# The attention's decay bias as a fourth product of the scores' matmul sum

## The chip, the cores and the metric

The kernel runs on one core of a Trainium2 chip. The metric is the device time of one execution in microseconds (us). Five engines run their own instruction streams in order and wait for each other on semaphores: PE (TensorE, matrix products), DVE (VectorE), ACT (ScalarE), POOL (GpSimd) and SP (SyncE, which here only issues DMAs).

## The reference, cut to what matters

Three layers follow each other: a causal attention with a decay bias, a mixture of eight experts whose gate is normalised eight times, and a two-matrix layer with softplus. The change lies in the attention alone:

```python
B, H, S, D = q.shape                     # 2, 8, 576, 64
scale = 1.0 / np.sqrt(D)                 # 1/8
scores = scale * np.matmul(q, k.transpose(0, 1, 3, 2))
causal = np.triu(np.ones((S, S), dtype=bool), k=1)
s_pos = np.maximum(s, 0.0)
cum = np.cumsum(s_pos, axis=-1)
bias = -(cum[:, :, :, None] - cum[:, :, None, :])
scores = np.where(causal, -1000000000.0, scores + np.minimum(bias, 0.0))
scores = scores - np.max(scores, axis=-1, keepdims=True)
attn = np.exp(scores)
attn = attn / (np.sum(attn, axis=-1, keepdims=True) + 1e-09)
return np.matmul(attn, v).astype(np.float32)
```

The bias of row r and column c is cum[c] - cum[r]. Where the mask lets a column through, it is never above zero, since cum only grows.

## The kernel before

Two heads form a pair (p = 0 to 7); head j of a pair stands on partitions 64j to 64j + 63 of q and k. The 576 rows of a head are cut into four blocks of 128 and a rest of 64. A unit (p, i) is row block i of both heads; i = 4 is the rest, both heads stacked on 128 partitions. So a pair has five units and the attention 40, numbered n = 0 to 39.

float32 operands are split into high bits and a rest (kh, kl, qh, ql), and the scores are the sum of three products, qh·kh + qh·kl + ql·kh, in PSUM (`scores`, L313 and L318; unit i = 0 takes one plain float32 product, L304). With c8 = 8·cum, DVE works out min(cum[c] - cum[r], 0) and the mask block by block into an SBUF tile `eb` (L366 and L367, for i = 4 L379 and L380). It needs c8 spread over all partitions (`cb`, a DMA from the DRAM scratch `c8d` that repeats each row 128 times, L223) and c8 as columns (`ccol`, made by TensorE transposes, L334 to L340). A custom DVE instruction (L371; L384 and L387 for i = 4) adds the scores to `eb` and takes the row's extreme; ACT takes the exponential (L399), DVE the sum's reciprocal (L408, L410), POOL scales the rows (L412), PE transposes them (L424, L430, L436), ACT takes them out of PSUM (L444), and PE multiplies by v (L456, L466).

The order is written by hand as a software pipeline. Step n issues, in this order: the last rest of a finished pair (Y), the scores of unit n + 1 (S), half a tile of the first expert's up-projection (U, L127, from step 28 on, four steps in five), the split of the next pair's k or q (K), v products of unit n - 5 (A), X, the evacuation of unit n - 4 (V), a piece of the first expert's weights (W), softmax of unit n with the reciprocals of unit n - 2 (B), the transposes of unit n - 3 (T), and the exponentials of unit n (E). The loads of the next pair follow at i = 1 (`load_rest`: cb, then v). After step 47 the experts' loop runs, in which PE has no pause.

PSUM has four score banks, so the scores of unit n + 1 wait for the row extremes of unit n - 1. The v tiles have two buffers, and SP issues in order: the v load of a pair stands in SP's queue until PE has done the last v product of the pair before the last one.

Of the kernel before, what the change touches and what calls it, by code (L numbers as in the profile page):

```python
# [10 lines left out]
F32 = mybir.dt.float32  # L11
# [9 lines left out]
def attention_moe_ffn(ctx, tc, q, k, v, s, w_gate, w1, w2, w_in, w_out, out):  # L21
# [41 lines left out]
    # The last layer's come as float64; as float32 they stand in DRAM scratch.  # L63
# [17 lines left out]
    def prep_steps(e, which, i, parts=1):  # L81
        """With more than one part, the rests are GpSimd's."""
        if e >= NE:
            return
        key = (e, which, i)
        t = raw_t.pop(key)
        hi = w_p.tile([P, WQ], F32R, tag=f"w{which}h", name=f"w{which}h")
        lo = w_p.tile([P, WQ], F32R, tag=f"w{which}l", name=f"w{which}l")
        c = KD if which == 1 else TQ
        wt[key] = (hi.rearrange("p (c n) -> p c n", c=c), lo.rearrange("p (c n) -> p c n", c=c))  # L90
        nc.scalar.activation(out=hi, in_=t, func=AF.Copy)  # L91
        for a in range(parts):
# [21 lines left out]
    def up_steps(e, g, ft, tag):  # L114
        """A generator: it stops halfway through the sum."""
# [28 lines left out]
        # a2: what 1 + a1 rounds away  # L144
# [17 lines left out]
    def down(e, g, t, tag):  # L162
        """A generator: it stops after each quarter of the sum."""
# [26 lines left out]
    with tc.manual_schedule():  # L190
        nc.scalar.preload_act_table_set("natural_log_exp_and_others")

# [1 line left out]
        with ExitStack() as att:  # L194
# [15 lines left out]
            def load(n):  # L210
                """Pair n // 2's k, then its q: both heads' rows."""
                p, r = divmod(n, 2)
                if p >= B * NP:
                    return
                b, hp = divmod(p, NP)
                x = ap2.tile([P, S], F32, tag="qk", name="qk", bufs=4)
                nc.sync.dma_start(out=x, in_=(q if r else k)[b, hp])
                qk_t.append(x)

            def load_rest(p):  # L220
                b, hp = divmod(p, NP)
                cb = ap2.tile([P, 2, S], F32, tag="cb", name="cb")
                nc.sync.dma_start(out=cb, in_=c8d[p:p + 1].to_broadcast([P, 2, S]))  # L223
                vv = ap2.tile([P, NB + 1, 2, D], F32, tag="vv", name="vv")
                hs = slice(2 * hp, 2 * hp + 2)
                nc.sync.dma_start(out=vv[:, :NB], in_=v[b, :NB * P, hs, :].rearrange("(c p) h d -> p c (h d)", p=P))
                nc.sync.dma_start(out=vv[:REM, NB], in_=v[b, NB * P:, hs, :])
                pair.setdefault(p, {}).update(vv=vv, cb=cb)
# [12 lines left out]
            c8d = dr.tile([B * NP, 2, S], F32, name="c8d")  # L241
            nc.sync.dma_start(out=c8d.rearrange("a j s -> (a j) s"), in_=c8)
# [8 lines left out]
            mask4 = ac.tile([P, REM], F32, name="mask4")  # L251
            nc.gpsimd.memset(mask4, 0.0)
            for j in range(2):
                r = slice(j * REM, (j + 1) * REM)
                nc.gpsimd.affine_select(out=mask4[r, :], in_=mask4[r, :], pattern=[[-1, REM]],
                                        compare_op=ALU.is_ge, fill=MASKED, base=0, channel_multiplier=1)

            ends = [[ac.tile([P, P], F32R, name=f"end{x}{y}") for y in "hl"] for x in range(2)]
            for x in ends:
                for y in x:  # L260
                    nc.gpsimd.memset(f(y), 0.0)

            def split(n, engine=nc.gpsimd):
                """Highest bits and the rest of load(n)."""
# [11 lines left out]
            def split_ends(p):  # L276
                """q's rows past the last whole block stand apart, head by head on the diagonal."""
# [16 lines left out]
            def scores(u):  # L294
# [3 lines left out]
                live[u] = dict(sc=sc)  # L298
                if i > 0:
                    kh, kl = t["kh"], t["kl"]  # L300
                else:
                    for j, x in enumerate(sc):
                        r = slice(j * D, (j + 1) * D)
                        nc.tensor.matmul(x[:, :P], qk_t[2 * p + 1][r, :P], qk_t[2 * p][r, :P], start=True, stop=True)  # L304
                    return
                if i < NB:
# [3 lines left out]
                    for n, (a, b) in enumerate(((qh, kh), (qh, kl), (ql, kh))):  # L310
                        for j, x in enumerate(sc):
                            r = slice(j * D, (j + 1) * D)
                            nc.tensor.matmul(x[:, :kp], a[r, qs], b[r, :kp], start=(n == 0), stop=(n == 2))  # L313
                else:
                    qh, ql = t["ends"]
                    for z, ks in ((sc[0][:, :S - 2 * P], slice(0, S - 2 * P)), (sc[1][:, :2 * P], slice(S - 2 * P, S))):
                        for n, (a, b) in enumerate(((qh, kh), (qh, kl), (ql, kh))):
                            nc.tensor.matmul(z, a, b[:, ks], start=(n == 0), stop=(n == 2))  # L318

            load_rest(0)  # L320
            ccol = ac.tile([P, NB, B * H], F32, name="ccol")
            ccol4 = ac.tile([P, B * H // 2], F32, name="ccol4")
            # the first row blocks' rows of c8, spread by TensorE
            cb0 = [ps.tile([P, 2, (i + 1) * P], F32, tag=f"y{i + 1}", name="cb0", bufs=1) for i in range(2)]

            def spread(i):
                for j in range(2):
                    nc.tensor.matmul(cb0[i][:, j, :], ident[:B * H, j:j + 1].to_broadcast([B * H, P]),
                                     c8[:, :(i + 1) * P], start=True, stop=True)

            spread(0)
            pc = ps.tile([P, NB + 1, B * H], F32, tag="tr", name="pc", bufs=2)
            for i in range(NB):
                nc.tensor.transpose(pc[:, i, :], c8[:, i * P:(i + 1) * P], ident[:B * H, :B * H])  # L334
            nc.tensor.transpose(pc[:REM, NB, :], c8[:, NB * P:], ident[:B * H, :B * H])
            spread(1)
            nc.vector.tensor_copy(ccol, pc[:, :NB, :])
            last = pc[:REM, NB, :].rearrange("p (a j) -> p j a", j=2)
            for j in range(2):
                nc.vector.tensor_copy(ccol4[j * REM:(j + 1) * REM, :], last[:, j, :])  # L340

# [9 lines left out]
            def softmax(u, before):  # L351
                """With `before`: the sums' reciprocals of the unit before, and what else waits."""
                p, i = u
                t, l = pair[p], live[u]
                cb, n = cb0[i] if p == 0 and i < 2 else t["cb"], 2 * p
                st = ap2.tile([P, 8], F32, tag="st", name="st", bufs=6)
                l["st"], l["eb"] = st, []
                if i < NB:
                    kk = (i + 1) * P
                    for j in range(2):  # L360
                        eb = eb_tile()
                        l["eb"].append(eb)
                        c, lo = ccol[:, i, n + j:n + j + 1], 0
                        if i > 1:
                            lo = i * P
                            nc.vector.tensor_scalar(eb[:, :lo], cb[:, j, :lo], c, 0.0, ALU.subtract, ALU.min)  # L366
                        nc.vector.scalar_tensor_tensor(out=eb[:, lo:kk], in0=cb[:, j, lo:kk], scalar=c,  # L367
                                                       in1=mask[:, W - kk + lo:], op0=ALU.subtract, op1=ALU.min)
                    for j, (eb, sc) in enumerate(zip(l["eb"], l["sc"])):
                        next(before, None)  # L370
                        nc.vector.tensor_tensor_reduce(eb[:, :kk], sc[:, :kk], eb[:, :kk], -0.125, BIG,  # L371
                                                       ALU.add, ALU.min, st[:, j:j + 1])
                else:
                    eb = eb_tile()
                    l["eb"].append(eb)
                    for j in range(2):
                        r = slice(j * REM, (j + 1) * REM)
                        c = ccol4[r, p:p + 1]
                        nc.vector.tensor_scalar(eb[r, :W], cb[r, j, :W], c, 0.0, ALU.subtract, ALU.min)  # L379
                        nc.vector.scalar_tensor_tensor(out=eb[r, W:], in0=cb[r, j, W:], scalar=c,  # L380
                                                       in1=mask4[r], op0=ALU.subtract, op1=ALU.min)
                    x, y = l["sc"]
                    next(before, None)
                    nc.vector.tensor_tensor_reduce(eb[:, S - 2 * P:], y[:, :2 * P], eb[:, S - 2 * P:], -0.125, BIG,  # L384
                                                   ALU.add, ALU.min, st[:, 4:5])
                    next(before, None)
                    nc.vector.tensor_tensor_reduce(eb[:, :S - 2 * P], x[:, :S - 2 * P], eb[:, :S - 2 * P], -0.125, BIG,  # L387
# [209 lines left out]
        # highest bits and rests side by side, their products are added up later  # L597
# [59 lines left out]
        # float64 words to float32; beyond float32's range they become 0 or its largest value.  # L657
        def convert(cv):
# [15 lines left out]
            for i, (_, dst) in enumerate(todo):  # L674
# [14 lines left out]
                # halves are rounded up: the highest bit that t has lost, times t's last place  # L689
# [8 lines left out]
        def turn(g):  # L698
            """The last layer's input: the experts' sum, transposed."""
# [73 lines left out]
def _parts(w, c):  # L773
    """[.., c * 128, n] in tiles with one run of memory for each partition: [.., 128, c, n]"""
# [5 lines left out]
def _columns(w, n):  # L780
    """[.., d, f] cut into blocks of n columns: [.., f / n, d, n]"""
# [4 lines left out]
def _pairs(a):  # L786
    """[B, H, S, D] as [B, H / 2, 2 * D, S]"""
# [33 lines left out]
```

## Time and profile before

| | |
|---|---|
| timed runs | 1143.37, 1143.65, 1145.00 us; median 1143.65 |
| span of the profiled execution, first to last instruction | 1142.8 us, 0.85 us below the median |
| busy in the span | PE 1120.3 us (98%), DVE 640.8 (56%), ACT 393.0 (34%), POOL 194.3 (17%) |
| attention, about 0 to 142 us | PE 123.7 us, DVE 123.0, ACT 94.7, POOL 84.7 |
| 8 loads of cb in it | 576 KB each, median 5.7 us from issue to landing |

The share of a whole span says little here: the attention is an eighth of it and has another limit than the experts. It is read by stretches of one pair.

### The profile page before, as it was taken

What the parts mean: (1) busy time and instruction counts of PE and PEld (TensorE: products, weight loads), DVE (VectorE), ACT (ScalarE), POOL (GpSimd) and SP (SyncE); (2) the same over time, 40 slices, a digit from 0 to 9 for tenths busy, and PEclk for the clock granted to TensorE, in tenths of its full rate; (3) what the DMA queues carried; (4) which work ended last, traced back from release to release, by engine and by line L of the source; (5) the groups of instructions that cost most, each with busy time, mean ns of one, the idle gap of its engine ahead of it and who ended that gap; (6) DMA issues with size and microseconds to landing.
All of it is one profiled execution on the core that took longest, in us unless ns stands there. A gap on an engine that the chain in (4) does not pass through costs nothing.

```text
span 1142.8 us, 15674 instructions
## 1 busy us (share of the span) xinstructions
PE 1120.3 (98%) x6037; PEld 993.1 (87%) x6037; DVE 640.8 (56%) x1316; ACT 393.0 (34%) x771; POOL 194.3 (17%) x234
## 2 busy tenths in 40 slices
PE   7789999999999999999999999999999999999998
PEld 5567788999999999999999999999999998999997
DVE  8998624644555465455546545554632357566653
ACT  5767622231223122122312212231221246565541
POOL 6675400000110111011011101101100012222220
PEclk9989999999999999999999999999999999999999
DMA  5432110220331223033122303312220112010001
GB/s 208 116 116 95 52 74 1 75 74 28 111 111 65 91 74 122 28 111 111 65 83 78 126 29 111 111 65 81 102 73 5 38 37 75 1 56 19 19 20 46
DMA packets 31210, 82.82 MB, mean 72 GB/s; under 512 B 5888, under 2 KB 10496, under 8 KB 31136
## 3 DMA queue, kind: packets, MB, share of 16 engines
q1 hardware_dynamic: 28576, 73.44, 19.7%
q0 software_dynamic: 2560, 8.39, 1.8%
q8 instruction: 47, 0.77, 0.3%
q14 instruction: 27, 0.22, 0.1%
HBM read 70.57 MB, written 10.78 MB: 71 GB/s over the span
## 4 chain that ended last, share of the span: by engine, by line
PE 92%; DVE 6%; issue 1%; DMA 1%; ACT 0%; ACTq 0%
PE ph L127 44%; PE py L174 44%; DVE eb L367 2%; DVE eb L371 1%; PE pv L456 1%; PE tr L430 1%; DVE eb L366 1%; PE sc L313 1%; DVE eb L379 1%; DVE st L408 0%; DVE eb L380 0%; PE pg L616 0%; PE px L703 0%; DMA cb<-c8d 0%; PE pv L466 0%
## 5 line engine op out<-in xcount | busy, mean ns | idle before, releaser
L127 PE MATMUL ph<-xh,w1h 128*128 128x384 f32 x960 | 325.2, 339 | 0.0
L127 PE MATMUL ph<-xl,w1h 128*128 128x384 f32 x960 | 322.4, 336 | 0.0
L127 PE MATMUL ph<-xh,w1l 128*128 128x384 f32 x960 | 322.4, 336 | 0.0
L133 DVE SCALAR_TENSOR_TENSOR hl<-ph,hh 128x384 fp32r<-128x384 f32 x192 | 106.6, 556 | 328.2 <-ACT hh L132 328.1
L174 PE MATMUL py<-w2h,hl 128*128 128x512 f32 x720 | 284.3, 395 | 0.0
L174 PE MATMUL py<-w2l,hh 128*128 128x512 f32 x720 | 283.6, 394 | 0.0
L174 PE MATMUL py<-w2h,hh 128*128 128x512 f32 x720 | 279.9, 389 | 0.0
L132 ACT ACTIVATE hh<-ph 128x384 fp32r<-128x384 f32 x192 | 94.5, 492 | 495.7 <-PE ph L127 495.5
L127 PEld LDWEIGHTS ph<-xh,w1h 128*128 128x128 f32 x960 | 180.3, 188 | 10.3 <-issue 0.7
L127 PEld LDWEIGHTS ph<-xl,w1h 128*128 128x128 f32 x960 | 180.3, 188 | 8.9
L127 PEld LDWEIGHTS ph<-xh,w1l 128*128 128x128 f32 x960 | 180.1, 188 | 0.0
L174 PEld LDWEIGHTS py<-w2h,hl 128*128 128x128 f32 x720 | 135.0, 187 | 28.6
L174 PEld LDWEIGHTS py<-w2l,hh 128*128 128x128 f32 x720 | 135.0, 187 | 22.5
L174 PEld LDWEIGHTS py<-w2h,hh 128*128 128x128 f32 x720 | 135.3, 188 | 22.0
L693 POOL TENSOR_TENSOR cm<-cm,ct 128x512 f32<-128x512 f32 x32 | 42.8, 1339 | 620.1 <-DVE ct L692 620.1
L147 POOL TENSOR_TENSOR a<-a,a 128x384 f32<-128x384 f32 x48 | 48.8, 1016 | 247.8 <-DVE a L145 247.8
L95 DVE TENSOR_TENSOR w2l<-raw,w2h 128x1024 fp32r<-128x1024 f32 x38 | 46.4, 1222 | 29.4 <-ACT w2h L91 29.4
L180 DVE SCALAR_TENSOR_TENSOR acc<-py,gate,acc 128x512 f32<-128x512 f32 x63 | 47.2, 749 | 19.5 <-PE py L174 19.4
L95 DVE TENSOR_TENSOR w1l<-raw,w1h 128x1024 fp32r<-128x1024 f32 x36 | 46.4, 1289 | 12.8 <-ACT w1h L91 11.8
L399 ACT ACTIVATE eb<-eb,st 128x128 f32<-128x128 f32 (+4 forms) x72 | 41.5, 579 | 31.9 <-DVE st L410 14.1
L412 POOL TENSOR_SCALAR eb<-eb,st 128x128 f32<-128x128 f32 (+4 forms) x72 | 43.2, 611 | 41.3 <-DVE st L410 27.5
L91 ACT ACTIVATE w2h<-raw 128x1024 fp32r<-128x1024 f32 x40 | 42.2, 1057 | 22.8 <-PE py L174 18.7
(146 smaller groups left out, 992.2 us busy)
## 6 DMA issues: line engine op xcount, KB each, us to landing
raw<-in_w SPq DMA_DIRECT2D x64, 512.0 KB, 5.5
f<-in_w_in SPq DMA_DIRECT2D x16, 512.0 KB, 4.4
f<-in_w_out SPq DMA_DIRECT2D x16, 512.0 KB, 3.5
wd<-cm POOLq DMA_DIRECT2D x32, 256.0 KB, 4.7
raw<-wd SPq DMA_DIRECT2D x16, 512.0 KB, 3.3
cb<-c8d SPq DMA_DIRECT2D x8, 576.0 KB, 5.7
qk<-in_k SPq DMA_DIRECT2D x8, 288.0 KB, 3.1
qk<-in_q SPq DMA_DIRECT2D x8, 288.0 KB, 3.2
```

Of the source, the lines that this page charges most:

```text
L91: nc.scalar.activation(out=hi, in_=t, func=AF.Copy)
L95: (nc.gpsimd if parts > 1 else nc.vector).tensor_tensor(out=lo[:, r], in0=t[:, r], in1=f(hi[:, r]), op=ALU.subtract)
L127: nc.tensor.matmul(ph, a, b, start=(n == 0), stop=(n == len(ops) - 1))
L132: nc.scalar.activation(out=hh, in_=ph, func=AF.Relu)
L133: nc.vector.scalar_tensor_tensor(out=hl, in0=ph, scalar=0.0, in1=f(hh), op0=ALU.max, op1=ALU.subtract)
L147: nc.gpsimd.tensor_tensor(out=a2, in0=a1, in1=a2, op=ALU.subtract)
L174: nc.tensor.matmul(py, x, y, start=(ft == 0 and n == 0), stop=(ft == NFT - 1 and n == 2))
L180: nc.vector.scalar_tensor_tensor(out=a, in0=py, scalar=gate_t[0][:, tt, e:e + 1], in1=a, op0=ALU.mult, op1=ALU.add)
L367: nc.vector.scalar_tensor_tensor(out=eb[:, lo:kk], in0=cb[:, j, lo:kk], scalar=c, in1=mask[:, W - kk + lo:], op0=ALU.subtract, op1=ALU.min)
L399: nc.scalar.activation(out=eb[:, :kk], in_=eb[:, :kk], func=AF.Exp, bias=st[:, j:j + 1], scale=-1.0, accum_out=st[:, 2 + j:3 + j])
L412: nc.gpsimd.tensor_scalar(eb[:, :kk], eb[:, :kk], st[:, 6 + j:7 + j], 1.0, ALU.mult, ALU.mult)
L693: nc.gpsimd.tensor_tensor(out=m, in0=m, in1=f(t), op=ALU.add)
```

## The change

The bias and the scores are both sums over products, so cum[c] - cum[r] is written as four more rows of a product. c8 is split into high bits and rest (`cs`, by ACT and DVE, once), and c8, its rest and both with the sign turned go to the DRAM scratch `c8d`. For each pair six small DMAs (`load_bias`) put two rows of 576 (or 64) values into the tiles bk, bq and be, whose other rows POOL has set to ones and zeros at the start (`init_bias`). `scores` then adds a fourth product, bq·bk (be·bk for i = 4), to each sum. DVE's bias blocks, the broadcast loads of cb and the columns `ccol` go; the custom instruction now adds the mask itself. The minimum with zero is no longer taken. The removed comments of the diff are left out here.

```diff
...
-                cb = ap2.tile([P, 2, S], F32, tag="cb", name="cb")
-                nc.sync.dma_start(out=cb, in_=c8d[p:p + 1].to_broadcast([P, 2, S]))
+                if p > 0:
+                    load_bias(p)
...
+            BB = 2
+            bq_t = [ac.tile([P, S], F32R, name=f"bq{x}") for x in range(BB)]
+            bk_t = [ac.tile([P, S], F32R, name=f"bk{x}") for x in range(BB)]
+            be_t = [ac.tile([P, P], F32R, name=f"be{x}") for x in range(BB)]
+
+            def init_bias(x):
+                for t in (bq_t[x], bk_t[x], be_t[x]):
+                    nc.gpsimd.memset(f(t), 0.0)
+                for j in range(2):
+                    for t, cols in ((bq_t[x], slice(0, S)), (bk_t[x], slice(0, S)),
+                                    (be_t[x], slice(j * REM, (j + 1) * REM))):
+                        nc.gpsimd.memset(f(t[j * D:j * D + 4, cols]), 1.0)
+
+            def load_bias(p):
+                for j in range(2):
+                    h = 2 * p + j
+                    nc.sync.dma_start(out=f(bk_t[p % BB][j * D + 2:j * D + 4, :]), in_=c8d[h, 0:2, :])
+                    nc.sync.dma_start(out=f(bq_t[p % BB][j * D:j * D + 2, :]), in_=c8d[h, 2:4, :])
+                    nc.sync.dma_start(out=f(be_t[p % BB][j * D:j * D + 2, j * REM:(j + 1) * REM]),
+                                      in_=c8d[h, 2:4, NB * P:])
...
-            c8d = dr.tile([B * NP, 2, S], F32, name="c8d")
-            nc.sync.dma_start(out=c8d.rearrange("a j s -> (a j) s"), in_=c8)
+            init_bias(0)
+            cs = [eb_tile(B * H, f"cs{x}").bitcast(F32R) for x in range(4)]
+            c8d = dr.tile([B * H, 4, S], F32, name="c8d")
+            for a, b in ((0, 2 * P), (2 * P, S)):
+                x = c8[:, a:b]
+                nc.scalar.activation(out=cs[0][:, a:b], in_=x, func=AF.Copy)
+                nc.scalar.activation(out=cs[2][:, a:b], in_=x, func=AF.Copy, scale=-1.0)
+                nc.vector.tensor_tensor(out=cs[1][:, a:b], in0=x, in1=f(cs[0][:, a:b]), op=ALU.subtract)
+                nc.vector.tensor_tensor(out=cs[3][:, a:b], in0=f(cs[0][:, a:b]), in1=x, op=ALU.subtract)
+            for x in range(4):
+                nc.sync.dma_start(out=c8d[:, x, :], in_=f(cs[x]))
+            load_bias(0)
...
-                        nc.tensor.matmul(x[:, :P], qk_t[2 * p + 1][r, :P], qk_t[2 * p][r, :P], start=True, stop=True)
+                        nc.tensor.matmul(x[:, :P], qk_t[2 * p + 1][r, :P], qk_t[2 * p][r, :P], start=True, stop=False)
+                    for j, x in enumerate(sc):
+                        r = slice(j * D, (j + 1) * D)
+                        nc.tensor.matmul(x[:, :P], bq[r, :P], bk[r, :P], start=False, stop=True)
...
-                    for n, (a, b) in enumerate(((qh, kh), (qh, kl), (ql, kh))):
+                    for n, (a, b) in enumerate(((qh, kh), (qh, kl), (ql, kh), (bq, bk))):
...
-                        for n, (a, b) in enumerate(((qh, kh), (qh, kl), (ql, kh))):
-                            nc.tensor.matmul(z, a, b[:, ks], start=(n == 0), stop=(n == 2))
+                        for n, (a, b) in enumerate(((qh, kh), (qh, kl), (ql, kh), (be, bk))):
+                            nc.tensor.matmul(z, a, b[:, ks], start=(n == 0), stop=(n == 3))
...
-            spread(0)
...
-                        if i > 1:
-                            lo = i * P
-                            nc.vector.tensor_scalar(eb[:, :lo], cb[:, j, :lo], c, 0.0, ALU.subtract, ALU.min)
-                        nc.vector.scalar_tensor_tensor(out=eb[:, lo:kk], in0=cb[:, j, lo:kk], scalar=c,
-                                                       in1=mask[:, W - kk + lo:], op0=ALU.subtract, op1=ALU.min)
...
-                        nc.vector.tensor_tensor_reduce(eb[:, :kk], sc[:, :kk], eb[:, :kk], -0.125, BIG,
+                        nc.vector.tensor_tensor_reduce(eb[:, :kk], sc[:, :kk], mask[:, W - kk:], -0.125, BIG,
...
```

Two places show how the instructions stand. The first is DVE, softmax of unit i = 3 (the v and norm work of other units stands between; st holds a row's extreme, sum and reciprocal). Before:

```order
L366 TENSOR_SCALAR eb<-cb,ccol 128x384
L367 SCALAR_TENSOR_TENSOR eb<-cb,ccol,mask 128x128
L366 TENSOR_SCALAR eb<-cb,ccol 128x384
L367 SCALAR_TENSOR_TENSOR eb<-cb,ccol,mask 128x128
L408 TENSOR_SCALAR st<-st 128x2
L371 ISA eb,st<-sc,eb 128x512
L371 ISA st 128x1
L410 RECIPROCAL st<-st 128x2
L371 ISA eb,st<-sc,eb 128x512
```

And in the changed kernel, where the line numbers are those of its own file:

```order
L412 TENSOR_SCALAR st<-st 128x2
L381 ISA eb,st<-sc,mask 128x512
L381 ISA st 128x1
L414 RECIPROCAL st<-st 128x2
L381 ISA eb,st<-sc,mask 128x512
```

The four bias instructions in front of the unit are gone; the custom instruction reads the mask where it read eb. The second place is SP's queue from one pair's v load to the bias of the next pair. Before:

```order
L226 DMA vv<-in_v 128x4x128
L227 DMA vv<-in_v 64x128
L78 DMA raw<-in_w 128x1024
L287 DMA end0h<-qh 64x64 x2
L287 DMA end0l<-ql 64x64 x2
L217 DMA qk<-in_k 128x576
L217 DMA qk<-in_q 128x576
L223 DMA cb<-c8d 128x1152
```

In the changed kernel:

```order
L226 DMA vv<-in_v 128x4x128
L227 DMA vv<-in_v 64x128
L78 DMA raw<-in_w 128x1024
L322 DMA end0h<-qh 64x64 x2
L322 DMA end0l<-ql 64x64 x2
L217 DMA qk<-in_k 128x576
L217 DMA qk<-in_q 128x576
L248 DMA bk_95<-c8d 2x576
L249 DMA bq_93<-c8d 2x576
L250 DMA be_97<-c8d 2x64
L248 DMA bk_95<-c8d 2x576
L249 DMA bq_93<-c8d 2x576
```

One DMA has become six (the sixth, be of the second head, follows). Before, it was DVE's softmax that waited for this load; now it is PE, whose scores stand first in a step.

## Rows read from the trace of the kernel before

**Rows 1.** The chain that ended last, in order of time: start, us, what.

```profile
142.17 4.36 PE ph L127 x24
```

**Rows 2.** Stretches: length, busy PE PEld DVE ACT POOL, PEclk, DMA share, GB/s.

```profile
32.36:48.36 16.00, 11.81 (x114) 8.46 (x113) 15.92 (x51) 11.46 (x31) 11.29 (x15) 1.00 0.47 131
48.36:64.46 16.10, 13.34 (x113) 9.51 (x114) 16.02 (x51) 11.28 (x31) 10.49 (x14) 0.89 0.40 130
64.46:79.65 15.19, 14.14 (x113) 10.26 (x113) 15.11 (x51) 11.87 (x32) 10.93 (x15) 0.78 0.43 138
...
96.54:111.86 15.32, 15.32 (x139) 11.92 (x138) 13.00 (x52) 11.19 (x33) 8.13 (x11) 1.00 0.20 63
```

**Rows 3.** Timeline of PE, 93 to 110 us: start, duration, instruction.

```profile
93.13 0.39 PE L318 MATMUL sc<-kh,end1h 128*128 128x320 f32 x1
...
96.96 0.44 PE L127 MATMUL ph<-xh,w1h 128*128 128x384 f32 x1
...
98.21 0.95 PE L466 MATMUL pv<-pt,vv 128*64 128x64 f32 x20
...
99.89 0.28 PE L313 MATMUL sc<-kl,qh 64*128 64x256 f32 x2
100.01 0.29 PE L313 MATMUL sc<-kh,ql 64*128 64x256 f32 x2
...
106.57 0.40 PE L313 MATMUL sc<-kl,qh 64*128 64x512 f32 x2
106.80 0.39 PE L313 MATMUL sc<-kh,ql 64*128 64x512 f32 x2
```

**Rows 4.** Groups of DVE, 32.36 to 79.65 us: busy, mean ns, idle before.

```profile
L367 DVE SCALAR_TENSOR_TENSOR eb<-cb,ccol,mask 128x128 f32<-128x128 f32 (+1 forms) x24 | 16.1, 691 | 0.0
...
L366 DVE TENSOR_SCALAR eb<-cb,ccol 128x256 f32<-128x256 f32 (+1 forms) x12 | 8.6, 717 | 0.0
...
L379 DVE TENSOR_SCALAR eb<-cb,ccol 64x512 f32<-64x512 f32 x6 | 3.3, 548 | 0.0
...
L380 DVE SCALAR_TENSOR_TENSOR eb<-cb,ccol,mask 64x64 f32<-64x64 f32 x6 | 2.3, 386 | 0.0
```

**Rows 5.** Timeline of PE, 20 to 147 us; in brackets the idle time before.

```profile
48.36 0.48 PE L304 MATMUL sc<-qk 64*128 64x128 f32 x2 [0.45 <-DVE st L371]
...
50.82 0.63 PE L424 MATMUL tr<-ident,eb 128*128 128x128 f32 x4 [0.42 <-ACT pt L444]
...
52.59 0.44 PE L456 MATMUL pv<-pt,vv 128*64 128x128 f32 x4 [0.37 <-DVE xl L530]
...
132.10 0.44 PE L456 MATMUL pv<-pt,vv 128*64 128x128 f32 x4 [1.29 <-DVE xl L530]
```

**Rows 6.** Timeline of SP's queue, 0 to 150 us: start, time to issue, DMA.

```profile
0.74 0.40 SPq L231 DMA_DIRECT2D s_sb<-in_s  x1
1.20 0.41 SPq L217 DMA_DIRECT2D qk<-in_k  x1
...
50.44 0.38 SPq L226 DMA_DIRECT2D vv<-in_v  x1
...
55.69 0.38 SPq L223 DMA_DIRECT2D cb<-c8d  x1
```

**Rows 7.** Timeline of all engines, 0 to 17 us.

```profile
1.26 0.52 POOL L248 MEMSET mask<- 128x512 f32 x1
...
4.78 0.33 SPq L242 DMA_DIRECT2D c8d<-c  x1
4.95 1.40 POOL L274 TENSOR_TENSOR kl<-qk,kh 128x576 fp32r<-128x576 f32 x1 [1.24 <-ACT kh L273]
...
7.21 0.34 SPq L223 DMA_DIRECT2D cb<-c8d  x1
...
14.31 0.89 POOL L412 TENSOR_SCALAR eb<-eb,st 128x128 f32<-128x128 f32 x2 [1.14 <-DVE st L410]
...
16.67 0.58 PE L304 MATMUL sc<-qk 64*128 64x128 f32 x1 [0.25 <-DVE st L371]
```

More of the change, by code (lines that the diff above doesn't have):

```diff
@@ L227, in load_rest @@
                 nc.sync.dma_start(out=vv[:REM, NB], in_=v[b, NB * P:, hs, :])
-                pair.setdefault(p, {}).update(vv=vv, cb=cb)
+                pair.setdefault(p, {}).update(vv=vv)
+            BB = 2
[16 more added lines that the diff above has]
+                                      in_=c8d[h, 2:4, NB * P:])
             s_sb = eb_tile(B * H, "s_sb")
@@ L250, in attention_moe_ffn @@
                                     compare_op=ALU.is_ge, fill=MASKED, base=0, channel_multiplier=1)
-            mask4 = ac.tile([P, REM], F32, name="mask4")
+            mask4 = ac.tile([P, S], F32, name="mask4")
             nc.gpsimd.memset(mask4, 0.0)
@@ L254, in attention_moe_ffn @@
                 r = slice(j * REM, (j + 1) * REM)
-                nc.gpsimd.affine_select(out=mask4[r, :], in_=mask4[r, :], pattern=[[-1, REM]],
+                nc.gpsimd.affine_select(out=mask4[r, W:], in_=mask4[r, W:], pattern=[[-1, REM]],
                                         compare_op=ALU.is_ge, fill=MASKED, base=0, channel_multiplier=1)
@@ L261, in attention_moe_ffn @@
                     nc.gpsimd.memset(f(y), 0.0)
+            for x in range(1, BB):
+                init_bias(x)
             def split(n, engine=nc.gpsimd):
@@ L298, in scores @@
                 live[u] = dict(sc=sc)
+                bq, bk, be = bq_t[p % BB], bk_t[p % BB], be_t[p % BB]
                 if i > 0:
@@ L309, in scores @@
                     qh, ql = t["qh"], t["ql"]
-                    for n, (a, b) in enumerate(((qh, kh), (qh, kl), (ql, kh))):
+                    for n, (a, b) in enumerate(((qh, kh), (qh, kl), (ql, kh), (bq, bk))):
                         for j, x in enumerate(sc):
                             r = slice(j * D, (j + 1) * D)
-                            nc.tensor.matmul(x[:, :kp], a[r, qs], b[r, :kp], start=(n == 0), stop=(n == 2))
+                            nc.tensor.matmul(x[:, :kp], a[r, qs], b[r, :kp], start=(n == 0), stop=(n == 3))
                 else:
@@ L316, in scores @@
                     for z, ks in ((sc[0][:, :S - 2 * P], slice(0, S - 2 * P)), (sc[1][:, :2 * P], slice(S - 2 * P, S))):
-                        for n, (a, b) in enumerate(((qh, kh), (qh, kl), (ql, kh))):
-                            nc.tensor.matmul(z, a, b[:, ks], start=(n == 0), stop=(n == 2))
+                        for n, (a, b) in enumerate(((qh, kh), (qh, kl), (ql, kh), (be, bk))):
+                            nc.tensor.matmul(z, a, b[:, ks], start=(n == 0), stop=(n == 3))
             load_rest(0)
[L321 to L329, printed above, removed]
-            spread(0)
[L332 to L340, printed above, removed]
             scores(units[0])
@@ L353, in softmax @@
                 p, i = u
-                t, l = pair[p], live[u]
-                cb, n = cb0[i] if p == 0 and i < 2 else t["cb"], 2 * p
+                l = live[u]
                 st = ap2.tile([P, 8], F32, tag="st", name="st", bufs=6)
@@ L359, in softmax @@
                     kk = (i + 1) * P
-                    for j in range(2):
+                    for j, sc in enumerate(l["sc"]):
                         eb = eb_tile()
                         l["eb"].append(eb)
-                        c, lo = ccol[:, i, n + j:n + j + 1], 0
-                        if i > 1:
-                            lo = i * P
-                            nc.vector.tensor_scalar(eb[:, :lo], cb[:, j, :lo], c, 0.0, ALU.subtract, ALU.min)
-                        nc.vector.scalar_tensor_tensor(out=eb[:, lo:kk], in0=cb[:, j, lo:kk], scalar=c,
-                                                       in1=mask[:, W - kk + lo:], op0=ALU.subtract, op1=ALU.min)
-                    for j, (eb, sc) in enumerate(zip(l["eb"], l["sc"])):
                         next(before, None)
-                        nc.vector.tensor_tensor_reduce(eb[:, :kk], sc[:, :kk], eb[:, :kk], -0.125, BIG,
+                        nc.vector.tensor_tensor_reduce(eb[:, :kk], sc[:, :kk], mask[:, W - kk:], -0.125, BIG,
                                                        ALU.add, ALU.min, st[:, j:j + 1])
@@ L375, in softmax @@
                     l["eb"].append(eb)
[L376 to L381, printed above, removed]
                     x, y = l["sc"]
                     next(before, None)
-                    nc.vector.tensor_tensor_reduce(eb[:, S - 2 * P:], y[:, :2 * P], eb[:, S - 2 * P:], -0.125, BIG,
+                    nc.vector.tensor_tensor_reduce(eb[:, S - 2 * P:], y[:, :2 * P], mask4[:, S - 2 * P:], -0.125, BIG,
                                                    ALU.add, ALU.min, st[:, 4:5])
                     next(before, None)
-                    nc.vector.tensor_tensor_reduce(eb[:, :S - 2 * P], x[:, :S - 2 * P], eb[:, :S - 2 * P], -0.125, BIG,
+                    nc.vector.tensor_tensor_reduce(eb[:, :S - 2 * P], x[:, :S - 2 * P], mask4[:, :S - 2 * P], -0.125, BIG,
                                                    ALU.add, ALU.min, st[:, 5:6])
```

## The prediction

> **What bounds the kernel now.** The chain that ended last is PE's from 142.17 us on [rows 1]; only the attention, before that, can move the end. I read it first by stretches of one pair. From 32 to 80 us DVE is busy for 15.92 of 16.00, 16.02 of 16.10 and 15.11 of 15.19 us, while ACT has 11.3 to 11.9, POOL 10.5 to 11.3 and PE 11.8 to 14.1 us [rows 2]: DVE paces the first half. From 96.54 on PE is busy for all of 15.32 us and DVE for 13.00: with the expert's up-projection between the units, PE paces the second half. PE's timeline dates the turn: the first-half pace holds until the scores of unit 29 (p = 5, i = 4) at 93.13, behind which the first up-projection follows [rows 3].
>
> **Part 1: DVE's bias blocks go.** Over three pairs they take 16.1 + 8.6 + 3.3 + 2.3 = 30.3 us [rows 4], 10.1 a pair. DVE's 15.9 a pair becomes about 5.8. Nothing is added on DVE in the loop: the custom instruction reads the mask in place of eb, in the same shape, and I cost that at nothing. DVE falls far below the others, so the question is what is late next.
>
> **Part 2: the pace of the first half without DVE.** Four candidates, a pair each:
> - ACT keeps all its work: (11.46 + 11.28 + 11.87)/3 = 11.5 us [rows 2].
> - POOL: (11.29 + 10.49 + 10.93)/3 = 10.9 us [rows 2].
> - PE at full clock: 15.32 us hold four pieces of up-projection; one takes 98.21 - 96.96 = 1.25 us [rows 3], so 15.32 - 5.0 = 10.3 us are attention. The fourth product costs, by start-to-start distances, 0.12 us for the two heads at 256 columns and 0.23 at 512 [rows 3]. Between these I take 0.12 for 128 columns, 0.17 for 384, and 0.15 and 0.12 for the stacked unit's 320 and 256. Sum 0.12 + 0.12 + 0.17 + 0.23 + 0.27 = 0.91 us: 11.2 a pair.
> - SP's ring: the scores of a pair now wait for the pair's bias rows, whose DMAs stand behind the v load in SP's queue, and that load waits for PE in the step of the scores of the pair before. From scores at 48.36 [rows 5] to the v load at 50.44 are 2.1 us, from there to the load of cb at 55.69 are 5.25 [rows 6]. PE needs the first five of six DMAs for the unit i = 0; at 0.46 us from issue to issue (0.74 to 1.20 [rows 6]) the fifth starts 1.8 us later, and a small transfer through DRAM took 7.21 - 4.78 = 2.4 us until its reader could go [rows 7]. Ring: 2.1 + 5.25 + 1.8 + 2.4 = 11.6 us.
>
> The four lie between 10.9 and 11.6. Where one engine paces, the others' waits hide; with four so near, each in order, part of their waits adds up. PE's waits that DVE's blocks don't cause, on ACT's evacuation and on xl, are 0.42 + 0.37 us in one pair [rows 5]. I take 11.5 + 0.8 = 12.3 us a pair; the floor is 11.5, the upper bound today's pace.
>
> Between the scores of unit 5 at 16.67 [rows 7] and those of unit 29 at 93.13 [rows 3] lie 24 steps, 4.8 pairs, 15.9 us each. At 12.3 they take 59.0 in place of 76.5 us: 17.5 us less.
>
> **Part 3: the start.** Two costs lie on the path to unit 5.
> - c8 must be split and go through DRAM. Before, its DMA starts at 4.78 [rows 7]; now four subtractions by DVE on 16 rows come first, 1.5 us at the 386 ns of the smallest group and 2.8 at the 691 of the largest [rows 4]. I take 1.5, since nothing else runs on DVE. The last of the four DMAs goes at 6.3, has landed at 8.7, the fifth bias DMA starts 1.8 later and takes 2.4: 12.9 us for the scores of unit 0, or up to 0.7 less where the issues overlap; I take 12.2.
> - POOL sets the bias tiles before its first kl. One set is six memsets of 576 columns, by the 0.52 us of the mask's 512 [rows 7], and three small ones: 3.6 us; two sets and the wider mask are about 7.5. POOL's first kl moves from 4.95 to about 11.5, and since the next kl and ql (1.4 us each [rows 7]) and the split by ACT stand before POOL's first scaling of rows, that goes from 14.31 to about 17.5, the first transposes to about 18.5, and the scores of unit 5, behind them on PE, to about 19.2 in place of 16.67. Lag 2.5 us, between 0 and 5.
>
> The spread by TensorE and the columns ccol go too; they lie before unit 0, which now waits for the DMAs anyway, so I count no gain.
>
> **Part 4: the second half.** PE paces it and gets the fourth product of units 29 to 39: two pairs at 0.91 and one stacked unit at 0.27, 2.1 us more. PE's one large pause, 1.29 us before 132.10, ends on xl by DVE, which stood behind the last bias blocks [rows 5]; it goes. Net 0.8 us more. From there on the same instructions run, only earlier.
>
> **Parts off the path.** The eight broadcasts of cb (576 KB each) go and 48 small DMAs come. Their price is in SP's ring; the bytes saved help raw and qk land, which nothing waits for long now, so zero, with 1 us either way.
>
> **Sum.** -17.5 + 2.5 + 0.8 = -14.2 us on the profiled span of 1142.8, which lies 0.85 below the median run: 1143.65 - 14.2 = 1129.5 us.
>
> **TensorE's clock** is the unknown. The granted clock was 1.00 in one pair of the first half, 0.89 and 0.78 in the next two, with PE pausing on DVE, and 1.00 where PE was never idle [rows 2]. [...]
>
> **Rivals.**
> 1. PE stays at a mixed clock. At the 0.78 of the third pair, 11.2 us of PE work become 14.4 a pair and PE paces. 4.8 × (15.9 - 14.4) = 7.2 less 3.3 gives 1139.8 us. For it: the two dips, and that the first half still has no up-projection to fill PE. Against it: where PE had 100% the clock stayed at 1.00, and PE now has 91% to do at that level.
> 2. ACT alone paces, without added waits, at 11.5, and the lag at the start hides behind it: 4.8 × 4.4 = 21 - 1.5 - 0.8 gives 1125 us. For it: the steps have one unit of slack everywhere. Against it: in-order waits of four engines.
> 3. Slower: the bias rows land late. PE stands in front of the scores of unit i = 0 until the fifth small DMA has landed, and everything behind it on PE (v products, transposes) stands too. The ring is 11.6 us at 2.4 us to land. It reaches today's pace at 6.7 us, and since 3.3 us are lost anyway, the change is slower once a transfer takes over 6.0: the ring is then above 15.2. At 7.4, as behind the raw weights and two loads of qk that stand in front in the queue, it would be 16.6, so 4.8 × 0.7 + 3.3 = 6.7 us slower, 1150 us. For it: cb took 5.7 us in the median. Against it: cb moved 576 KB, these some 5 KB.
> 4. It doesn't remove the limit: the row extremes still run on DVE behind the reciprocals of unit n - 2, which wait for ACT, and the pace stays near 15.5: 4.8 × 0.4 - 3.3 is about 1 us slower, 1145 us. Against it: ACT has 11.5 us to do in 16 and so keeps two units ahead once DVE lets it.
>
> **How the numbers follow.** Chances: the forecast (pace 12 to 13, 1126 to 1134 us) 0.55; rival 1 and everything between 13 and 15 (1134 to 1142) 0.25; rival 2 and better (1120 to 1126) 0.12; rival 3 0.05; rival 4 0.03. The time is the forecast's, 1129.5 us. The range for 8 in 10 runs from 1121, below rival 2, to 1139, which takes in most of rival 1. A difference counts from 0.2% on, 2.3 us, about what a measurement of this kernel can tell from no change: faster 0.91 (the forecast, rival 2, nearly all of rival 1), the same 0.04, slower 0.05.
>
> **What would show it.** Right: DVE about 6 us busy per pair until the first up-projection and ACT over 90%; scores of unit 29 near 78 us (19.2 + 59.0); granted clock 0.95 or more; bias products 0.23 us for two heads at 512 columns; unit 5's scores near 19 us; the second half within 1 us of the 49 us between 93.13 and 142.17 [rows 1, 3]. Rival 1 shows as L127-free pairs of 14 us and more with PE without pauses at a low clock; rival 3 as PE waiting on the bias DMAs before each unit i = 0; rival 4 as ACT idle on DVE. The prediction is wrong if the pace lies outside 11.3 to 13.8 us a pair, or if something after the attention starts to wait on loads that no longer have their lead.

## The result, and the profile after

The changed kernel takes 1125.82 us (median of four runs: 1125.42, 1125.47, 1126.17, 1128.16) beside 1144.13 for the kernel before on the same chip: ratio 0.9844, 95% interval 0.9830 to 0.9858. The forecast was 1129.5, range 1121 to 1139. The gain is 18.3 us by the medians; the profiled spans (1142.8 and 1123.6 us) differ by 19.2.

The page of the changed kernel has PE on 98% of the chain, and DVE at 585.9 us, 54.9 less than before.

```profile
## 1 busy us (share of the span) xinstructions
PE 1107.6 (99%) x6104; PEld 987.7 (88%) x6104; DVE 585.9 (52%) x1189; ACT 393.1 (35%) x775; POOL 197.1 (18%) x252
...
PE 98%; POOL 1%; ACT 0%; issue 0%; DVE 0%; POOLq 0%; ACTq 0%
```

These stretches of the changed kernel, from one pair's first scores to the next's, answer to [rows 2] (length, then busy time of PE, PEld, DVE, ACT, POOL with counts, PEclk, DMA share, GB/s). The fifth holds one piece of up-projection, the sixth several.

```profile
19.49:30.49 11.00, 11.00 (x105) 8.38 (x104) 8.46 (x40) 10.96 (x33) 11.00 (x17) 1.00 0.26 82
30.49:41.87 11.38, 11.38 (x125) 8.85 (x124) 7.06 (x34) 11.13 (x32) 10.32 (x16) 1.00 0.45 133
41.87:53.45 11.58, 11.41 (x124) 8.85 (x123) 7.42 (x34) 11.07 (x32) 9.19 (x14) 1.00 0.44 131
53.45:64.83 11.38, 11.38 (x124) 8.85 (x123) 5.63 (x27) 10.94 (x31) 10.07 (x16) 1.00 0.42 133
64.83:77.53 12.70, 12.70 (x130) 9.96 (x129) 7.85 (x33) 10.68 (x33) 9.53 (x14) 1.00 0.40 120
77.53:93.73 16.20, 16.20 (x148) 12.79 (x147) 7.35 (x35) 11.40 (x33) 7.67 (x11) 1.00 0.09 25
```

PE's column equals the length in all but one stretch, where 0.17 us are missing: from unit 5 on PE paces the attention, the first half too. DVE has fallen from 15.9 us a pair to between 5.6 and 8.5. ACT and POOL are close behind PE. The granted clock is 1.00 in all six, where [rows 2] had 0.89 and 0.78.

PE's timeline dates the same points as [rows 3, 5, 7]: the scores of unit 5, of unit 29, and the first piece of the expert loop that PE runs to the end.

```profile
19.49 0.71 PE L340 MATMUL sc<-qk 64*128 64x128 f32 x3
...
73.85 0.39 PE L357 MATMUL sc<-kh,end1h 128*128 128x320 f32 x1
...
122.17 0.95 PE L470 MATMUL pv<-pt,vv 128*64 128x64 f32 x20
123.05 0.44 PE L127 MATMUL ph<-xh,w1h 128*128 128x384 f32 x1
```

| stretch | before | after | difference | forecast |
|---|---|---|---|---|
| start to the scores of unit 5 | 16.67 | 19.49 | +2.8 | +2.5 |
| unit 5 to unit 29, 4.8 pairs | 76.46 (15.9 a pair) | 54.36 (11.33 a pair) | -22.1 | -17.5 |
| unit 29 to the end of the attention | 49.0 | 49.2 | +0.2 | +0.8 |
| sum | | | -19.1 | -14.2 |

So the direction and the order of the terms held, and the large term was too small by 4.6 us.

### The profile page after: what moved, and what is told of

The parts are those of the page before. It is cut to its first block, busy times and chain, and to the rows that moved or that the text cites. A ratio compares the mean times of both kernels' runs of the same rounds, so it can differ in the third digit from the quotient of the medians.

```text
span 1123.6 us, 15723 instructions
## 1 busy us (share of the span) xinstructions
PE 1107.6 (99%) x6104; PEld 987.7 (88%) x6104; DVE 585.9 (52%) x1189; ACT 393.1 (35%) x775; POOL 197.1 (18%) x252
## 4 chain that ended last, share of the span: by engine, by line
PE 98%; POOL 1%; ACT 0%; issue 0%; DVE 0%; POOLq 0%; ACTq 0%
PE ph L127 45%; PE py L174 44%; PE pv L460 2%; PE sc L352 2%; PE tr L434 1%; PE tr L428 1%; PE sc L357 1%; PE pv L470 1%; PE tr L440 0%; PE pg L620 0%; PE px L707 0%; PE sc L340 0%; POOL bk L243 0%; POOL bq L243 0%; ACT eb L403 0%
## 5 line engine op out<-in xcount | busy, mean ns | idle before, releaser
L151 ACT ACTIVATE hh<-a 128x384 fp32r<-128x384 f32 x48 | 25.3, 527 | 71.2 <-DVE a L150 71.2
```

Of the source, the lines that this page charges most:

```text
L151: nc.scalar.activation(out=hh, in_=a3, func=AF.Copy)
```

## Experiments

The kernel before was timed beside every experiment, with medians of 1143.8 to 1144.7 us; the ratios are to these. The changed kernel was timed once, beside 1144.13 us.

### 1. All of DVE's bias blocks back, with nobody reading them

```diff
+for j in range(2):
+    ...                                          # c is a column of ones, lo = i * P for i > 1
+    if i > 1: nc.vector.tensor_scalar(eb[:, :lo], mask4[:, :lo], c, 0.0, ALU.subtract, ALU.min)
+    nc.vector.scalar_tensor_tensor(out=eb[:, lo:kk], in0=mask4[:, lo:kk], scalar=c,
+                                   in1=mask[:, W - kk + lo:], op0=ALU.subtract, op1=ALU.min)
 # the same two operations for i = 4; the fourth product and the small transfers stay
```

> The changed kernel, with dead VectorE instructions of the old bias blocks' number and shapes put back ahead of each unit's row extremes (their results are overwritten); the fourth product and the small DMAs stay. Theory (VectorE's blocks were the whole of the first half's limit): a pair takes 15.9 us again, so 4.8 x (15.9 - 11.3) = 22 us more than the changed kernel, 1148 us, and the granted clock dips again where PE pauses. Rival (what helped was getting rid of the 576 KB broadcasts, or of their place in SP's queue): stays within 4 us of 1126.

Measured: 1148.99 us, ratio 1.0042 (1.0025 to 1.0059). Two stretches of it:

```profile
32.00:48.00 16.00, 13.07 (x117) 9.73 (x113) 15.92 (x50) 11.77 (x31) 11.11 (x15) 0.89 0.32 95
48.00:64.00 16.00, 14.78 (x125) 11.29 (x123) 15.92 (x50) 11.26 (x31) 10.39 (x15) 0.79 0.31 95
```

DVE is at 15.92 of 16.00 again, as in [rows 2], and the whole gain is gone, with 4.6 us lost on top (beside 1144.36) for what the new form adds. From one pair's first scores to the next's it is 15.90 us from 36.54 on and 16.12 from 52.44 on, as expected. The low clock is back too, 0.89 and 0.79. So the blocks' time on DVE was the limit, and neither the broadcasts of cb nor any other removed part had a share that shows.

### 2. Only the first kind of block back (4.0 of 10.1 us a pair)

The diff is that of the first experiment without its second operation.

> The same with only the tensor_scalar half of the dead blocks, 4.0 us a pair by the rows of before (8.6 + 3.3 over three pairs). VectorE then has about 7.1 + 4.0 = 11.1 us of work in a pair of 11.3, as near to the pace as ScalarE. Theory A (the pace is the largest engine total alone, near ties hide): 1126 us, no more than 1 us over the changed kernel. Theory B (the forecast's: engines near the pace add some of their waits, 0.8 us a pair): 4.8 x 0.8 = 3.8 us more, 1130 us.

Measured: 1132.18 us, ratio 0.9895 (0.9880 to 0.9910), past both expectations and nearer to the second. The stretches of its pairs say something else:

```profile
19.86:33.85 13.99, 12.93 (x103) 9.57 (x104) 12.41 (x44) 11.44 (x33) 12.36 (x17) 0.88 0.19 56
33.85:45.23 11.38, 11.38 (x124) 8.85 (x124) 10.42 (x39) 11.13 (x32) 10.27 (x14) 1.00 0.45 133
45.23:57.19 11.96, 11.44 (x124) 8.88 (x124) 11.34 (x44) 10.98 (x32) 9.79 (x14) 1.00 0.41 127
57.19:68.57 11.38, 11.38 (x124) 8.85 (x123) 9.32 (x33) 10.91 (x31) 10.63 (x16) 1.00 0.43 134
68.57:83.05 14.48, 13.11 (x131) 10.15 (x130) 10.94 (x40) 10.76 (x33) 10.11 (x15) 1.00 0.32 104
```

With PE, ACT, DVE and POOL all between 9.3 and 11.4 us, the second and the fourth pair still take 11.38 us, PE's own time. A near tie costs nothing there. The loss stands in single places, against the changed kernel's stretches: 0.4 us in the third pair, 1.8 in the fifth with its piece of up-projection, 3.0 in the first. In that one PE waits twice on DVE, for 0.19 us and then for 0.84, and behind that runs at a granted clock of 0.59 from 24 to 28 us:

```profile
22.51 0.77 PE L352 MATMUL sc<-kh,qh 64*128 64x256 f32 x2 [0.84 <-DVE st L423]
```

So my even charge of 0.8 us a pair for near ties has no counterpart in the rows.

### 3. Without the fourth product

This kernel leaves the bias out of the scores; all else, the small transfers too, stays.

```diff
-for n, (a, b) in enumerate(((qh, kh), (qh, kl), (ql, kh), (bq, bk))):
+for n, (a, b) in enumerate(((qh, kh), (qh, kl), (ql, kh))):
 # likewise for i = 0 and i = 4
```

> The changed kernel without the fourth product (the bias is left out of the scores); all DMAs, splits and memsets stay. Theory (PE's work is the pace from unit 5 on): the second half loses 2.1 us, and the first half 0.91 us a pair as far as ScalarE (11.0 to 11.1 busy) lets it, between 0.2 and 0.9 x 4.8 = 1 to 4.4 us: 1119.5 to 1122.7 us. Rival (ScalarE is the pace of the first half, PE only looks full): 1123.7 us, unit 5 to unit 29 unchanged at 54.4 us.

Measured: 1121.66 us, ratio 0.9803 (0.9789 to 0.9818), between the two expectations and inside the first one's range. The pairs show which engine comes next:

```profile
32.21:42.89 10.68, 10.55 (x114) 7.98 (x113) 7.17 (x34) 10.68 (x31) 8.95 (x13) 1.00 0.45 140
42.89:53.93 11.04, 10.57 (x115) 7.99 (x114) 7.20 (x34) 10.86 (x32) 9.56 (x15) 1.00 0.44 139
```

PE needs 10.55 us without and 11.38 with the fourth product: 0.83 a pair, forecast 0.91. Now ACT's 10.68 fill the first of these pairs' 10.68, and ACT paces, with PE 0.1 us behind; in the second PE waits 0.47 us for ACT. ACT's floor is therefore 10.7 to 10.9 us and not 11.5, and in the changed kernel PE alone sets 11.38.

By the medians the fourth product costs 1125.82 - 1121.66 = 4.2 us. The profiled run of this kernel took 1122.69 us and understates it: unit 5 to unit 29 took 53.77 us, only 0.6 less than in the changed kernel, because the pair before those two was longer than the changed kernel's 11.00:

```profile
19.41:32.21 12.80, 12.80 (x95) 9.37 (x94) 10.01 (x34) 10.79 (x33) 11.28 (x17) 1.00 0.24 73
```

PE has fewer products there and no pause, yet until about 26 us they are spaced wider than in the changed kernel, 0.32 us for two heads' 384 columns where it has 0.17, under a recorded 1.00 (see the last section). The sum alone, near the rival's unchanged 54.4, would have misled; the pairs behind it decide.

### 4. SP's ring

```diff
-for j in range(2):
+for j in list(range(2)) * (2 if p > 1 else 1):   # load_bias: each small transfer twice
```

> The changed kernel with each of the six small bias transfers of pairs 2 to 7 issued twice (same rows, same values; nothing else differs). In the changed kernel SP's ring per pair (scores, two v loads, bias loads, q and k loads, splits) measured nearly as long as the pair. Theory A (SP's ring is a second limit that nearly touches, six more issues of 0.3 us make it about 13.2 us against PE's 11.4): the pairs 3 and 4 take about 13.2 us each and one more loses about 0.7, some 4 to 5 us, 1130. Theory B (PE's instructions alone set the pace and SP has slack): 1125.8, the time of the changed kernel, with pairs of 11.4 us.

Measured: 1132.71 us, ratio 0.9900 (0.9883 to 0.9916): lengthened like this, the ring is the limit. PE's waits and three pairs:

```profile
44.48 0.29 PE L343 MATMUL sc<-bk,bq 64*128 64x128 f32 x1 [0.60 <-DMA bq<-c8d]
...
57.33 0.29 PE L343 MATMUL sc<-bk,bq 64*128 64x128 f32 x1 [0.60 <-DMA bq<-c8d]
...
69.85 0.29 PE L343 MATMUL sc<-bk,bq 64*128 64x128 f32 x1 [0.89 <-DMA bq<-c8d]
70.64 0.29 PE L343 MATMUL sc<-bk,bq 64*128 64x128 f32 x1 [0.50 <-DMA bq<-c8d]
```

```profile
42.94:55.81 12.87, 11.95 (x125) 9.11 (x124) 7.47 (x34) 11.07 (x32) 9.14 (x14) 1.00 0.43 119
55.81:68.47 12.66, 11.92 (x125) 9.11 (x124) 5.63 (x28) 10.93 (x32) 10.04 (x16) 1.00 0.39 121
68.47:85.74 17.27, 15.88 (x130) 12.15 (x130) 7.33 (x34) 11.11 (x33) 9.41 (x14) 0.80 0.28 90
```

The third and fourth pairs take 12.87 and 12.66 where 13.2 were expected, 1.3 us each over the changed kernel's. The fifth loses 4.6 us where 0.7 were expected: its two waits make 1.4, and PE goes on at a mean clock of 0.80. That is why the time went past the expected 1130. Another 1.1 us went in pair 1, whose rows are issued as in the changed kernel: PE waited 0.34 and 0.37 us for them and the pair took 12.09 us for 11.00, so these rows land only just in time.

That the pairs came out near 13.2 is in part luck, for the edit lengthens the ring by more than six issues. SP stood between the two rounds, and the transfer that PE needs went 3.35 us behind its first copy, not 1.8:

```profile
52.41 0.25 SPq L249 DMA_DIRECT2D bq<-c8d  x1
...
54.16 0.22 SPq L248 DMA_DIRECT2D bk<-c8d  x1
...
55.76 0.25 SPq L249 DMA_DIRECT2D bq<-c8d  x1
```

So 3.35 us more cost 1.3, and some 2 us of slack were there before. The changed kernel's own SP queue says nearly the same:

```profile
43.34 0.40 SPq L226 DMA_DIRECT2D vv<-in_v  x1
...
48.83 0.29 SPq L248 DMA_DIRECT2D bk<-c8d  x1
...
50.29 0.25 SPq L249 DMA_DIRECT2D bq<-c8d  x1
```

From the scores at 41.87 the v load follows after 1.47 us, the first bias transfer 5.49 after that, the fifth 1.46 later. With the forecast's 2.4 us to land that would be 10.8 us. But here PE could go at 57.33, 1.57 us behind the issue at 55.76; with that the ring is some 10.0 us, 1.4 under the pace (an estimate; forecast 11.6). Three of the four gaps between the small issues are 0.3 us, not 0.46.

### 5. The start: POOL's memsets

```diff
-for x in range(1, BB):
-    init_bias(x)
 ...
 split_ends(0)
+for x in range(1, BB):
+    init_bias(x)
 load(4)
```

> The changed kernel with GpSimd's memsets of the second set of bias tiles placed behind the first split of k. Theory (the start's lag is GpSimd's memsets ahead of kl, ql and the first scaling of rows): kl 3.8 us earlier, the first scaling about 1.8 us earlier, since the memsets still stand ahead of the next kl: scores of unit 5 near 17.7 instead of 19.5 us, 1124.0 us. Rival (c8's way through DRAM sets the start): unchanged, 1125.8 us.

Measured: 1125.24 us (1124.07 to 1128.16), ratio 0.9839 (0.9822 to 0.9855); no difference from the changed kernel that can be told. Two of the four runs did meet the expected 1124.0 (1124.07 and 1124.15); the only one with a profile took 1126.34. Its scores of unit 5 do come at 17.74, 1.75 us sooner, as expected. But the bias rows of pair 1, behind 1.6 MB of q, k and weights, don't come as much sooner, and PE waits for them:

```profile
17.74 0.49 PE L338 MATMUL sc<-qk 64*128 64x128 f32 x4
19.04 0.29 PE L341 MATMUL sc<-bk,bq 64*128 64x128 f32 x1 [0.81 <-DMA bq<-c8d]
19.64 0.29 PE L341 MATMUL sc<-bk,bq 64*128 64x128 f32 x1 [0.30 <-DMA bq<-c8d]
```

Behind these waits PE was busy without a pause, but at a lower clock, and pair 1 took 13.62 us in place of 11.00:

```profile
20.00:22.00 2.00, 2.00 (x18) 1.47 (x18) 1.62 (x11) 2.00 (x9) 2.00 (x4) 0.84 0.13 29
22.00:24.00 2.00, 2.00 (x12) 1.67 (x12) 0.38 (x3) 1.91 (x6) 1.63 (x2) 0.50 0.56 155
24.00:26.00 2.00, 2.00 (x21) 1.39 (x18) 1.19 (x6) 1.17 (x5) 2.00 (x4) 0.81 0.48 174
```

### 6. The start in another order, twice

First, with one memset for bk in place of three, the memsets behind the first split and the six transfers ahead of the big loads:

```diff
 ...
+init_bias(1)
+load_bias(1)
 load(4)
 load(5)
 load_next()
 load_next()
```

> The changed kernel with the start in another order: the memsets of the second bias set go behind POOL's first split, bk's takes one memset to 1.0 in place of three, and the second pair's six bias transfers are issued ahead of the q, k and weight loads instead of behind them. [...]

Measured: 1129.06 us (1127.95 to 1130.81), ratio 0.9872 (0.9857 to 0.9887), slower than the changed kernel by 3.2 us. PE had no wait for the bias rows, and yet pair 1 took 16.60 us. ACT and then PE in its timelines:

```profile
20.41 1.06 ACT L91 ACTIVATE w1h<-raw 128x1024 fp32r<-128x1024 f32 x1 [4.35 <-DMA raw<-in_w]
```

```profile
23.20 0.69 PE L459 MATMUL pv<-pt,vv 128*64 128x128 f32 x4 [4.00 <-ACT pt L447]
```

The weight load had become the late one. ACT is in order, so its copy of weights, which nothing needs yet, held up the exponentials and evacuations behind it. With the two `load_next()` ahead of `init_bias(1)` and the loads of q and k last:

> The second start order with one more move: the two weight loads (512 KB each) are issued first, then the second bias set's memsets and six small transfers, then the q and k loads of the third pair. In the order without this move ACT waited 4.35 us (16.06 to 20.41) for the first weight load, behind 0.9 MB of other loads, and PE stood 4.0 us for ACT's copy. Theory A (that wait was its whole loss; the q and k of the third pair have slack): the weights land before ACT comes to them at 16.1, the bias rows before 17.4; scores of unit 5 at 17.4, those of unit 10 at 28.4 to 29.0 (30.49 in the changed kernel), time 1123.6. Theory B (some other transfer is late then, v or the bias rows): pair 1 again over 13 us and a time of 1126 or more.

Measured: 1123.10 us (1122.96 to 1123.18), ratio 0.9813 (0.9797 to 0.9830): the fastest of the versions that keep the bias, 2.7 us under the changed kernel, with all four runs under its lowest. The two were not timed beside each other; the intervals of their ratios meet at 0.9830. PE in its timeline:

```profile
16.79 0.67 PE L427 MATMUL tr<-ident,eb 128*128 128x128 f32 x2 [0.60 <-POOL eb L415]
17.39 0.49 PE L337 MATMUL sc<-qk 64*128 64x128 f32 x4
28.12 0.49 PE L337 MATMUL sc<-qk 64*128 64x128 f32 x4
```

ACT comes to its weights at 15.98 without a wait, unit 5 starts at 17.39 and pair 1 takes 10.73 us: theory A.

### 7. Products of ones ahead of the first scores

```diff
+wm = ps.tile([P, P], F32, tag="tr", name="wm", bufs=2)
+for _ in range(26):
+    nc.tensor.matmul(wm, ones, ones, start=True, stop=True)
 scores(units[0])
```

> The changed kernel with 26 products of ones (128x128, results not read) on PE ahead of the first scores, in the stretch from 1.6 to about 10 us in which PE waits for data. In the changed kernel the score products from 10.2 to 16.9 us run at the 1.2 GHz level by their spacing (384 columns in 0.32 us) and PE starts the fifth unit's transposes at 18.88. [...] Theory B (POOL bounds the start: its first scaling of probabilities starts at 18.45 behind the memsets and splits): the products are faster but the scores of unit 5 stay within 0.4 us of 19.49, and the time is 1125.2.

Measured on the changed kernel: 1125.42 us (1124.93 to 1127.05), ratio 0.9841 (0.9826 to 0.9856), unit 5's scores at 19.07, 0.42 sooner: theory B. On the two other start orders:

> Both together: the 26 products of ones ahead of the first scores and the start in the other order. [...]

> The same with the 26 products of ones on PE ahead of the first scores. [...]

Measured: 1129.01 us against 1129.06 without the products, and 1124.96 (1122.75 to 1125.58) against 1123.10. The products win nothing that lasts. On the two other orders the score products did run faster (two heads' 384 columns in 0.18 us where it was 0.32 without the products of ones), and PE then stood 1.52 and 1.14 us for POOL's first scaling: POOL's chain, not PE's clock, bounds the start. In the last kernel POOL itself was sooner, so that unit 5's scores came at 16.55, 0.84 us before the 17.39 without the products; but ACT, busy for all of the next 11.50 us, held pair 1, and unit 10's came at 28.05, beside 28.12 without the products. On the changed kernel the clock didn't even stay up:

```profile
10.30:11.50 1.20, 1.10 (x10) 0.70 (x8) 0.55 (x4) 0.19 (x1) 1.16 (x4) 1.00 0.11 34
13.70:14.50 0.80, 0.73 (x8) 0.73 (x10) 0.07 (x1) 0.00 (x0) 0.80 (x2) 0.84 0.20 75
14.50:17.30 2.80, 2.80 (x16) 1.98 (x14) 2.38 (x11) 2.40 (x8) 1.25 (x2) 0.50 0.88 307
```

Ahead of the second stretch PE waited 2.29 us for POOL's kl, and the scores behind that wait ran at a granted clock of 0.50.

## Why the prediction was right, and where its sizes were off

The limit, its removal and the order of the terms were forecast rightly. The size was not: 1125.82 us lies in the range but just under the forecast's own band of 1126 to 1134 (0.55), in the one that had 0.12. The pace of 11.33 us is below the stated floor of 11.5 and only just inside the 11.3 to 13.8 that the prediction set itself, and unit 29 came at 73.85 us and not near 78.

- **Part 1** held: DVE's bias blocks, 10.1 us a pair, were the limit, shown both ways by experiment 1. The custom instruction did cost the same with the mask (669 and 682 ns at 512 columns). DVE was forecast at about 5.8 us and has 5.6 to 8.5, too far below the others to matter.
- **Part 2** is the mis-sized term: 12.3 us a pair forecast, 11.33 measured (54.36 over 4.8 pairs), which is 4.6 us of the time. Two pieces of it failed. "The floor is 11.5" took ACT's busy time under DVE's pace for what ACT needs. Experiment 3 has it at 10.68 us with the same work; in [rows 2] ACT was busy for 11.46, with five waits between its instructions, where each one's tail counts in full (one wait in the changed kernel's pair from 30.49 on). The instructions themselves got no shorter (a 128x512 evacuation took 586 ns before, 603 in the changed kernel). But back to back, the next starts about 0.1 us before the one before has ended, as the timeline of the changed kernel shows: 48.40 + 0.20 is behind 48.49.

```profile
48.40 0.20 ACT L403 ACTIVATION_READ_ACCUMULATOR eb<-eb,st 128x1 f32 x1
48.49 0.68 ACT L308 ACTIVATE qh<-qk 128x576 fp32r<-128x576 f32 x1
```

  The second piece, 0.8 us of waits that add up between near ties, came from waits that existed under DVE's pace [rows 5]; one of the two, 0.37 us on xl, ends on DVE, and for the like wait in Part 4 the prediction itself named the bias blocks. The changed kernel has 0.17 us of waits in one pair and none in the two beside it; experiment 2 shows them at single places. SP's ring, too, was put too high, at 11.6 for some 10.0 (experiment 4). So the four were not that near each other; PE's own candidate, 11.2, was the right floor (11.38).
- **The fourth product** was priced right: 0.83 us a pair for 0.91 (experiment 3).
- **Part 3** was right at +2.8 for +2.5, and in the main by the mechanism named, POOL's memsets ahead of its first kl: that kl went at 12.34 us (forecast 11.5), and moving the second set's memsets won 1.75 us (experiment 5), with one memset for bk 2.1 (experiment 6). Where the other 0.7 lies was not tried. c8's way was not it: the bias products of unit 0 were done at 11.5, sooner than forecast, and PE then waited 2.00 us for POOL's kl. That this lag could be won back was not in the forecast; winning it took two more moves, since each one made another load late.
- **Part 4**: +0.2 for +0.8. From unit 29's scores to the end of the attention PE was busy for 47.48 of 48.97 us before; now it is for all of 49.19. So the fourth product added 1.71 us there (forecast 2.1), and 1.49 us of pauses went (1.29). Before and after:

```profile
93.13:142.10 48.97, 47.48 (x440) 37.55 (x437) 35.07 (x130) 32.60 (x86) 22.81 (x31) 1.00 0.17 50
```

```profile
73.85:123.04 49.19, 49.19 (x462) 39.55 (x459) 19.51 (x88) 32.85 (x86) 21.78 (x31) 1.00 0.16 48
```
- **Rivals.** Rival 1 did not come: with PE hardly ever idle, 0.17 us in the 34.34 from 30.49 to 64.83, the clock stayed at 1.00. The number of transposes on PE doesn't tell this from the stretches with dips: the 26 of the pair from 30.49 to 41.87 take 3.8 of its 11.38 us, at a clock of 1.00; 25 in each of the two stretches of experiment 1, with PE pausing, stood beside 0.89 and 0.79. Rival 2 came nearest in time (1125), but with the wrong engine: PE paces, not ACT. Rival 3's mechanism is real and has a margin of 1.4 to 2 us a pair here (experiment 4), less in pair 1; it came true in experiment 5, for that pair. Rival 4 did not come.

## What to carry to other kernels

When the pacing engine is relieved, take the next floor from work that runs back to back: an engine's busy time among waits overstated ACT's by 7% here. Near ties needed no flat surcharge here; look for the single places where PE waits, and at the clock behind them. And a load or memset moved ahead can make another one late, so follow every in-order queue it passes before counting the gain (experiment 6).

## What the runs showed of the hardware

- **Short pauses and the clock.** PE waits of 0.81 and 0.30 us (experiment 5), of 0.89 and 0.50 (experiment 4) or of 0.19 and 0.84 (experiment 2) were followed by stretches at a lower granted clock: 0.50 from 22 to 24 us, 0.50 from 72 to 78 and 0.59 from 24 to 28. Others as long were not: the 0.60 in each of the two pairs before, in experiment 4, at 1.00; 0.20, 0.24 and 0.93 between 69 and 74 us of experiment 2, where the clock stayed at 1.00; and 4.2 us of pauses in the first pair of [rows 2], 1.40 the longest, also at 1.00. So the length of a pause doesn't settle it, and what does, these runs don't show. The time goes with the clock: the changed kernel's runs had mean clocks of 1.000 (1125.42, 1125.47), 0.999 (1126.17) and 0.998 (1128.16).
- **The start of the record.** In the changed kernel the first scores ran at the lower rate although the record grants 1.00. The timeline has two heads' products over 384 columns 0.32 us apart, 1.2 columns per ns, as in experiment 7 at a granted 0.50 (from 14.52 to 14.84), and the same products of the next pair only 0.17 apart, 2.2 to 2.3 columns per ns:

```profile
14.91 0.53 PE L352 MATMUL sc<-kl,qh 64*128 64x384 f32 x2
15.23 0.53 PE L352 MATMUL sc<-kh,ql 64*128 64x384 f32 x2
...
23.18 0.34 PE L352 MATMUL sc<-kl,qh 64*128 64x384 f32 x2
23.35 0.34 PE L352 MATMUL sc<-kh,ql 64*128 64x384 f32 x2
```

  In the profiled run of experiment 3 the second two are still 0.32 us apart, at 24.71 and 25.03, which made its pair 1 long. The 1.2 GHz of the first expectation of experiment 7 is this spacing of 0.32 us; the profiles give the clock only as a share of full speed. A clock of 1.00 in the first stretches of a record is therefore to be checked by the spacing of the products.
- **POOL beside DVE.** POOL's scaling of 128 columns took 445 ns on average beside the dead blocks of experiment 1 (four of them, from 36.54 to 68.56 us), and 376 in the changed kernel (six, from 30.49 to 64.83). But the kernel of experiment 3, which has no such blocks either, shows 390 ns (six, from 32.21 to 64.64), so the blocks are not the whole difference; how much is theirs was not tried.
